# Block 3's first product by seven products too, with seven sums of W_in on GpSimd

## The chip, the cores and the metric

The kernel runs on one core of one Trainium2 chip. The metric is the device time of one execution in microseconds. Before the change it is 192.94 us, the median of three runs (192.56 to 193.59). The engines are named as in the profile: PE is the matmul engine (PEld its weight loads), DVE is VectorE, ACT is ScalarE, POOL is GpSimd, SP is SyncE, which here only issues DMAs.

## The reference

A decayed linear attention (4 batches, 8 heads, 768 positions, head size 64) feeds a two-layer network with the Mish function between its layers:

```
state = gamma * state + k_t (outer) v_t;   y_t = q_t . state / sqrt(64)      # per head
x = y as [3072, 512]
h = x @ w_in        # [512, 2048]
g = h * tanh(softplus(h))
out = g @ w_out     # [2048, 512]
```

The kernel takes and gives float32 and multiplies in float16, with float32 sums in PSUM.

## The kernel before, in words

The 3072 rows are 24 chunks of 128. Block 0 has four chunks (512 rows); blocks 1 to 10 have two each (256 rows). For a block the kernel makes the attention rows, transposed, as the tile `xt`; then the first product `h = x @ w_in` with Mish behind it, which leaves `g`; then the second product `g @ w_out`, whose results go through `osb` to memory. While a block is in its products, PE also makes the scores (`at`), outer products (`u_ps`) and attention outputs (`y_ps`) of the next blocks. All is placed by hand: the order of the calls in the source is the order on every engine's queue, and each queue runs strictly in order.

The second product has two forms. The plain form is one matmul per piece of the inner dimension. The form by seven products (Strassen's scheme in Winograd's variant) cuts each operand into four quarters, makes seven half-size products instead of eight, and needs sums of quarters: of `g` (`gsum`, lines 866 to 879), and of w_out (`tmat`, `weight_sums`, L838). Block 0 uses seven products for half of its inner dimension (`first_out`, L750); its sums of `g` come from `first_sums` (L724) and lie in two of the tiles named `wsum`. Blocks 1 to 3 use `seven` (L985), blocks 4 to 10 `full_out` (L1082).

The first product has two forms too. Blocks 0 to 3 use the plain `g1` (L695): for blocks 1 to 3 eight calls of eight 256-column matmuls, each call followed by one ACT Mish (L714). Blocks 4 to 10 use `full_in` (L905): seven products, in two halves p, each of eight 128-column matmuls, 112 in all (L917). It needs four sums of `xt` (`x_sums`, L899, DVE) and sixteen sums of w_in, four for each of four tiles `wsum` (`in_sums`, L881). In the kernel before DVE makes all sixteen, two in block 1 and seven in each of blocks 2 and 3, one behind each `g1` call named in `SUMS_AT`. `full_in` uses more ACT work than `g1`: copies of partial results out of PSUM (L954, L940) beside the Mish.

The weights come in as float32 and are cast to float16: w_in by `cast_win` (L211; L220 and L226 on DVE, the first piece on POOL and ACT), w_out by `cast_wout` (L239, L241). These casts stand on DVE's queue between the sums of block 0, and PE uses each of them soon after.

POOL's work is the casting and scaling of q, k and v, chunk by chunk (`casts_qk` L437 and L440, `casts_v` L447; for block 1 L317). A one-column copy into `summed` (L1443, L1404) stands ahead of a group of them to hold it back until DVE has made a certain sum. When q and k of a chunk are cast, SP issues a DMA transpose (`turn_by_dma`, L452), whose result `qkt` PE needs for that chunk's scores. SP also issues all loads and nearly all stores, in the order of the calls (`turn_four` L1429 for blocks 2's time, `second_of` L1398 later).

`HALVED` and the variable `wide` in `g1` split some matmuls into two of half the columns, with the weights loaded for each: in block 0 the last seven `g1` calls (28 matmuls of 512 columns become 56 of 256), in block 6 sixteen matmuls of the second product.

Of the kernel before, what the change touches and what calls it, by code (L numbers as in the profile page):

```python
# [9 lines left out]
FP16 = mybir.dt.float16  # L10
# [6 lines left out]
def kernel(  # L17
# [677 lines left out]
    def g1(blk, u):  # L695
        nt = BLOCKS[blk] * C
        per = TB // nt
        h_ps = g1_bank(blk, u)
        for j in range(per):
            s, f = divmod(u * per + j, FPS)  # L700
            for bp in range(NBP):
                wide = 2 * C if u >= NFB - 7 else nt
                for at in range(0, nt, wide):
                    cols = slice(at, at + wide)
                    nc.tensor.matmul(  # L705
                        h_ps[:, j, cols], wins[s][f // 2][:, bp, f % 2 * P:(f % 2 + 1) * P],
                        xts[blk][:, bp, cols], start=(bp == 0 and at == 0), stop=(bp == NBP - 1),
                        skip_group_check=blk == 0)
# [5 lines left out]
        nc.scalar.activation(gt, h_ps, AF.Mish, scale=inv_boost3)  # L714
        for j in range(per):
            gts[blk, u * per + j] = gt[:, j]
# [7 lines left out]
    def first_sums():  # L724
        s = [win_sum_tile(j).rearrange("p a b c -> p (a b) c") for j in range(2)]
        s1, s2, s3, s4 = (s[i // 2][:, i % 2 * FPS:(i % 2 + 1) * FPS] for i in range(4))
        lo, hi = gtiles[0, 0][:, :FPS], gtiles[0, 1][:, :FPS]
        n = TB // 2
        add, sub = ALU.add, ALU.subtract
        return (s1, s2, s3, s4), [  # L730
            lambda: nc.vector.tensor_tensor(s3, lo[:, :, :n], lo[:, :, n:], op=sub),
            lambda: nc.vector.tensor_tensor(s1, lo[:, :, n:], hi[:, :, n:], op=add),
            lambda: nc.vector.tensor_tensor(s2, s1, lo[:, :, :n], op=sub),
            lambda: nc.vector.tensor_tensor(s4, hi[:, :, :n], s2, op=sub),
        ]
# [144 lines left out]

    def in_sums(j):  # L881
        t = win_sum_tile(j)
        (a11, a12), (a21, a22) = [
            (x[:, :2], x[:, 2:]) for x in (wins[j // 2][j % 2], wins[2 + j // 2][j % 2])]
        sub = ALU.subtract
        return [
            lambda: nc.vector.tensor_tensor(t[:, 0], a21, a22, op=ALU.add),
            lambda: nc.vector.tensor_tensor(t[:, 1], t[:, 0], a11, op=sub),
            lambda: nc.vector.tensor_tensor(t[:, 2], a11, a21, op=sub),
            lambda: nc.vector.tensor_tensor(t[:, 3], a12, t[:, 1], op=sub),  # L890
        ]
# [6 lines left out]

    def x_sums(blk, part):  # L899
        ((b11, b12), (b21, b22)), t = x_views(blk)  # L900
        sums = ((t[0], b12, b11), (t[1], b22, t[0]), (t[2], b22, b12), (t[3], b21, t[1]))
        for to, a, b in sums[2 * part:2 * part + 2]:
            nc.vector.tensor_tensor(to, a, b, op=ALU.subtract)

    def full_in(blk, last):  # L905
# [38 lines left out]

        def banks():
            return [single("h_ps", p).rearrange("p (f c) -> p f c", f=n) for p in two]

        pa, pf, m5 = [], [], []
        for p in two:
# [7 lines left out]
            m5.append(kept(pf[p]))  # L957
        if not last:
            u = held[blk + 1][1]
            g = first[blk + 1]  # L960
            for j in range(2):
                us[g + j] = u[:, :, j]
        for p in two:
            mm(pa[p], s(p, 2), t[1])
            nc.vector.tensor_tensor(pf[p], pa[p], m5[p], op=ALU.add)  # L965
            mm(pm[p], a(p, 0, 1), b[1][0])
            mish(p, 0, 0, pm[p])
            if not last:
                (mid_of, state_of)[p](g)
        h22 = []  # L970
        for p in two:
            mm(pa[p], s(p, 3), t[2])
            h22.append(kept(pa[p], m5[p]))
            if not last and p == 1:
# [10 lines left out]
    def seven(blk, masks, hooks):  # L985
# [63 lines left out]
        if blk < ONE:  # L1049
# [10 lines left out]
            call(hooks[2][1:])  # L1060
            mm(pl, a(1, 1), t(4), True)
            done(1, 0, pl, u3)
        else:
            call(hooks[0])
# [7 lines left out]
            mm(pe, s(4), b(1, 1))  # L1072
            x_sums(blk + 1, 0)
# [4 lines left out]
            x_sums(blk + 1, 1)  # L1078
        for i in range(2):
            stores.append((1 + i, out_rows(blk, i), osb[i]))  # L1080

    def full_out(blk, last):  # L1082
# [48 lines left out]
        px = pxps.tile([P, hf], FP32, name="o_ps", tag="px")  # L1131
        halved = HALVED.get(blk, (0, 0))
        mm(px, a(0, 0), b(0, 0), True, halved=halved[0])
# [12 lines left out]
        else:  # L1146
# [5 lines left out]
            pb = bank()  # L1152
            mm(pb, a(0, 1), b(1, 0), True)
            if later is None:
# [16 lines left out]
        done(1, 1, px, m5)  # L1171
        mm(pe, s(4), b(1, 1))
        if not last:
            x_sums(new, 0)
        done(0, 1, pe, u2)
# [4 lines left out]
        cols = slice(0, hf // 2 if last else hf)  # L1180
        mm(px, a(1, 1), t(4), cols=cols)
        if not last:
            x_sums(new, 1)
        done(1, 0, px, cols=cols)
# [28 lines left out]
    def first_block():  # L1213
# [70 lines left out]
        for s in range(1, NSL):  # L1284
            cast_win(s)

        def cast_qk():
# [110 lines left out]
    def second_of(blk):  # L1398
        g = first[blk] + 6
        load, ahead = (load_qk, -1) if blk + 1 == DEFER else (load_to, 0)  # L1400
        if blk != DEFER:
            load(g + 3 + ahead)
        if g < NCK:
            nc.gpsimd.tensor_copy(summed, xts[blk + 1][:, 3, TB - 1:])  # L1404
# [3 lines left out]
            casts_v(g + 1)  # L1408
        if blk == ONE or g >= NCK:
            store_due(NFB)  # L1410
# [65 lines left out]
    for blk in range(1, len(BLOCKS)):  # L1476
# [7 lines left out]
        if blk == 1:  # L1484
            for j in (0, 2, 1, 3):
                input_sums.extend(in_sums(j))
        for u in range(NFB // 2):
            g1(blk, u)
# [6 lines left out]
            elif u in SUMS_AT[blk]:  # L1495
                input_sums.pop(0)()
        later = blk + 2 if blk == ONE else None
        hooks = [([(leave, blk + 1)] if later is not None else []) + [(retain, blk + 1, later)],
# [38 lines left out]
```

## Time and profile before

| | us |
|---|---|
| median of three runs | 192.94 (192.56 to 193.59) |
| the profiled execution, its own time | 192.31 |
| its span, first to last instruction | 190.5 |
| PE busy | 184.8 (97% of the span) |
| DVE busy | 143.1 (75%) |
| ACT busy | 105.8 (56%) |
| POOL busy | 72.2 (38%) |
| mean granted TensorE clock | 0.999 of full speed |

Some 2 us of an execution lie outside the span. Three views are used below. The page gives busy shares and the chain that ended last. The chain in order of time gives the start of each piece, its length and what it was; pieces of one line are merged, and "x48" is the number of instructions. The timeline of an engine gives start, length, line, operation, output and input, the shape and the count; a bracket at the end tells the idle time before the group and what ended it. Matmul starts in the timeline stand some 0.15 us ahead of the chain's, since matmuls overlap.

### The profile page before, as it was taken

What the parts mean: (1) busy time and instruction counts of PE and PEld (TensorE: products, weight loads), DVE (VectorE), ACT (ScalarE), POOL (GpSimd) and SP (SyncE); (2) the same over time, 40 slices, a digit from 0 to 9 for tenths busy, and PEclk for the clock granted to TensorE, in tenths of its full rate; (3) what the DMA queues carried; (4) which work ended last, traced back from release to release, by engine and by line L of the source; (5) the groups of instructions that cost most, each with busy time, mean ns of one, the idle gap of its engine ahead of it and who ended that gap; (6) DMA issues with size and microseconds to landing.
All of it is one profiled execution on the core that took longest, in us unless ns stands there. A gap on an engine that the chain in (4) does not pass through costs nothing.

```text
span 190.5 us, 7643 instructions
## 1 busy us (share of the span) xinstructions
PE 184.8 (97%) x3310; PEld 162.3 (85%) x3310; DVE 143.1 (75%) x294; ACT 105.8 (56%) x201; POOL 72.2 (38%) x100
## 2 busy tenths in 40 slices
PE   7898999999999999999999999999999999999993
PEld 7656478888888888888998998998998998988982
DVE  0778469886977878988798698696697698676862
ACT  3366766264552552553684584584683673873650
POOL 5182000487508745940573634624534710000000
PEclk9999999999999999999999999999999999999999
DMA  4999999999999999899999997891899970301103
GB/s 147 310 303 350 382 387 376 293 330 226 189 237 294 172 235 238 129 266 234 220 186 317 156 202 165 214 200 39 194 174 244 219 172 3 114 3 53 62 3 112
DMA packets 84210, 38.82 MB, mean 204 GB/s; under 512 B 58192, under 2 KB 78288, under 8 KB 84176
## 3 DMA queue, kind: packets, MB, share of 16 engines
q1 hardware_dynamic: 83888, 38.22, 87.1%
q8 instruction: 26, 0.43, 1.0%
q10 hardware_dynamic: 288, 0.11, 0.4%
q14 instruction: 8, 0.07, 0.1%
HBM read 27.31 MB, written 6.29 MB: 176 GB/s over the span
## 4 chain that ended last, share of the span: by engine, by line
PE 93%; DMA 3%; DVE 1%; ACT 1%; issue 0%; SPq 0%; DVEq 0%
PE h_ps L917 23%; PE o_ps L1103 23%; PE h_ps L705 18%; PE o_ps L1007 10%; PE o_ps L762 7%; PE y_ps L609 3%; DMA qfirst<-in_q_dram 3%; PE u_ps L503 1%; PE at L495 1%; PE t_ps L267 1%; PE y_ps L396 1%; PE h_ps L687 1%; PE at L466 1%; PE at L347 1%; DVE qk L279 1%; PE u_ps L368 0%
## 5 line engine op out<-in xcount | busy, mean ns | idle before, releaser
L705 PE MATMUL h_ps<-xt,win 128*128 128x256 f16 (+1 forms) x276 | 34.3, 284 | 0.0
L705 PEld LDWEIGHTS <-win 128*128 128x128 f16 x276 | 26.7, 98 | 6.2 <-DVE win L220 0.3
L714 ACT ACTIVATE g<-h_ps 128x512 f16<-128x512 f32 x38 | 22.7, 597 | 15.2 <-PE h_ps L705 15.2
L917 PE MATMUL h_ps<-xt,wsum 128*128 128x128 f16 x448 | 29.6, 219 | 0.0
L929 ACT ACTIVATE g<-h_ps 128x512 f16<-128x512 f32 x42 | 24.2, 597 | 5.6 <-PE h_ps L917 5.6
L917 PEld LDWEIGHTS <-wsum 128*128 128x128 f16 x448 | 26.2, 98 | 0.0
L917 PE MATMUL h_ps<-xt,win 128*128 128x128 f16 x336 | 24.8, 219 | 0.0
L1103 PEld LDWEIGHTS <-gsum 128*128 128x128 f16 x232 | 21.5, 98 | 2.6
L1103 PE MATMUL o_ps<-tmat,gsum 128*128 128x256 f16 (+1 forms) x176 | 21.5, 268 | 0.0
L917 PEld LDWEIGHTS <-win 128*128 128x128 f16 x336 | 20.8, 98 | 0.2
L440 POOL TENSOR_TENSOR qk<-kf,qvs 128x512 f16<-128x512 f32 x18 | 18.9, 1052 | 2.5 <-DMA kf<-in_k_dram 2.5
L447 POOL TENSOR_TENSOR v<-vf,qvs 128x512 f16<-128x512 f32 x18 | 18.6, 1050 | 2.6 <-DMA vf<-in_v_dram 2.5
L437 POOL TENSOR_TENSOR qk<-qf,qvs 128x512 f16<-128x512 f32 x18 | 19.1, 1062 | 1.3 <-PE u_ps L368 1.3
L1103 PEld LDWEIGHTS <-g 128*128 128x128 f16 x184 | 16.5, 98 | 1.6
L667 ACT CAST xt<-y_ps 128x512 f16<-128x512 f32 x16 | 10.8, 738 | 11.1 <-PE y_ps L609 9.9
L965 DVE TENSOR_TENSOR h_ps<-h_ps,hsum 128x512 f32<-128x512 f32 x14 | 9.7, 695 | 9.2 <-PE h_ps L917 9.1
L1443 POOL COPY summed<-gsum 128x1 f16<-128x1 f16 x7 | 1.6, 233 | 36.8 <-DVE gsum L879 29.4
L954 ACT COPY h_ps<-h_ps 128x512 f32<-128x512 f32 x14 | 8.2, 583 | 12.4 <-issue 8.4
L1103 PE MATMUL o_ps<-wout,g 128*128 128x256 f16 (+1 forms) x120 | 14.5, 265 | 0.0
L1113 ACT COPY snap<-o_ps 128x256 f32<-128x256 f32 (+1 forms) x22 | 8.2, 373 | 11.0 <-PE o_ps L1103 11.0
L1126 DVE TENSOR_TENSOR osb<-o_ps,snap 128x256 f32<-128x256 f32 (+1 forms) x22 | 9.1, 415 | 4.2 <-ACT snap L1113 2.8
L942 DVE TENSOR_TENSOR hsum<-h_ps,hsum 128x512 f32<-128x512 f32 x14 | 9.6, 687 | 0.7 <-PE h_ps L917 0.2
(130 smaller groups left out, 334.0 us busy)
## 6 DMA issues: line engine op xcount, KB each, us to landing
out_dram<-osb SPq DMA_DIRECT2D x22, 256.0 KB, 3.9
qf<-in_q_dram SPq DMA_DIRECT2D x18, 256.0 KB, 4.8
kf<-in_k_dram SPq DMA_DIRECT2D x14, 256.0 KB, 6.0
vf<-in_v_dram SPq DMA_DIRECT2D x14, 256.0 KB, 5.3
wt<-in_moe_w_out_dram SPq DMA_DIRECT2D x6, 512.0 KB, 8.4
vf<-in_v_dram SPq DMA_DIRECT2D x20, 128.0 KB, 3.7
wi<-in_moe_w_in_dram SPq DMA_DIRECT2D x4, 512.0 KB, 8.3
wi<-in_moe_w_in_dram SPq DMA_DIRECT2D x2, 1024.0 KB, 11.1
```

The source lines that it names most:

```text
L437: nc.gpsimd.tensor_tensor(in_place(q16.rearrange("p (w x) d -> p w x d", x=2)), by_head(qf), scale_by_head(qs_two[:, heads]), op=ALU.mult)
L440: nc.gpsimd.tensor_tensor(k16.rearrange("p (y w) d -> p w y d", y=2), kf.rearrange("p (w y) d -> p w y d", y=2), boosts.rearrange("p (w y) ...
L447: nc.gpsimd.tensor_tensor(cast[g][2], loaded.pop(g)[2], vs[g % 2].unsqueeze(2).broadcast_to((P, H, D)), op=ALU.mult)
L667: nc.scalar.copy(dst[:, :, x], src)
L705: nc.tensor.matmul(h_ps[:, j, cols], wins[s][f // 2][:, bp, f % 2 * P:(f % 2 + 1) * P], xts[blk][:, bp, cols], start=(bp == 0 and at == 0) ...
L714: nc.scalar.activation(gt, h_ps, AF.Mish, scale=inv_boost3)
L762: nc.tensor.matmul(banks[ij][:, t], x(f)[:, t * P:(t + 1) * P], w(f), start=ij in open_banks, stop=f == fs[-1], skip_group_check=True)
L917: nc.tensor.matmul(o_ps[:, f], w(f // 2, k)[:, f % 2 * P:(f % 2 + 1) * P], x[:, k], start=begin and f == 0 and k == 0, stop=k == 1, skip_g ...
L929: nc.scalar.activation(gt[:, f:f + n, j * C:(j + 1) * C], src, AF.Mish, scale=inv_boost3)
L965: nc.vector.tensor_tensor(pf[p], pa[p], m5[p], op=ALU.add)
L1007: nc.tensor.matmul(o_ps[:, cols], x(f), w(f)[:, cols], start=first and z == 0, stop=z == n - 1, skip_group_check=True)
L1103: nc.tensor.matmul(o_ps[:, c:c + wide], x(f), w(f)[:, c:c + wide], start=first and f == 0 and c == cols.start, stop=f == n - 1, skip_group ...
```

## The change

- Block 3 is made a block like 4 to 10 in its first product: `full_in` instead of eight `g1` calls (`FULL = (3,)`). In block 3 `full_in` takes its extra PSUM banks from the early pool, carries out the state step of block 3 and the scores of block 4 within it (`both`), and orders its products a little otherwise. Block 2's second product makes block 3's `x_sums` on DVE.
- The sixteen sums of w_in must therefore be made by the end of block 2. DVE makes nine (two in block 1, seven in block 2). POOL makes seven: the four of tile 0 in block 0, right behind its part of the w_in casts and ahead of the casts for block 1, and three in block 1, behind six q, k and v casts.
- The sums of `g` in block 0 move from the `wsum` tiles to a third buffer of `g`, as `wsum` is written earlier.
- The halved matmuls: those of block 0 and block 6 are gone; blocks 4, 5, 7 and 8 get 16, 12, 8 and 24.
- SP's order: in `turn_four` two stores and the five loads of chunk 14 now stand ahead of the transpose of chunk 13; in `second_of` of block 3 two stores stand ahead of the transpose of chunk 15; the deferred loads of v come one block earlier (`DEFER` 5 for 6).

```diff
-    HALVED, DEFER = {6: (8, 8)}, 6
-    SUMS_AT = {1: (4, 5), 2: range(7), 3: range(7)}
+    HALVED = {4: (0, 0, 0, 8, 8), 5: (8, 4, 0, 0, 0), 7: (0, 0, 0, 0, 8), 8: (8, 8, 8, 0, 0)}
+    DEFER = 5
+    FULL, SUMS_AT = (3,), {1: (4, 5), 2: range(7)}
...
-                wide = 2 * C if u >= NFB - 7 else nt
-                for at in range(0, nt, wide):
...
     def first_sums():
-        s = [win_sum_tile(j).rearrange("p a b c -> p (a b) c") for j in range(2)]
-        s1, s2, s3, s4 = (s[i // 2][:, i % 2 * FPS:(i % 2 + 1) * FPS] for i in range(4))
+        s = gp.tile([P, 4, FPS, TB // 2], FP16, name="g", tag="g", bufs=3)
+        s1, s2, s3, s4 = (s[:, i] for i in range(4))
...
-    def in_sums(j):
+    def in_sums(j, on=None):
+        on = on or nc.vector
...
-            lambda: nc.vector.tensor_tensor(t[:, 0], a21, a22, op=ALU.add),
+            lambda: on.tensor_tensor(t[:, 0], a21, a22, op=ALU.add),
...
         def banks():
+            if blk < BACK:
+                t = atps.tile([P, 2, n, C], FP32, name="h_ps", tag="at")
+                return [t[:, p] for p in two]
...
-            mm(pm[p], a(p, 0, 1), b[1][0])
-            mish(p, 0, 0, pm[p])
-            if not last:
+            if not both:
+                mm(pm[p], a(p, 0, 1), b[1][0])
+                mish(p, 0, 0, pm[p])
+            if not settled:
                 (mid_of, state_of)[p](g)
+        if both:
+            leave(blk)
+            for p in two:
+                mm(pm[p], a(p, 0, 1), b[1][0])
+            for p in two:
+                mish(p, 0, 0, pm[p])
...
+        if blk < BACK:
+            get_ready(blk + 1)
         sums_a(blk, 0)
...
@@ in seven()
+            if blk + 1 in FULL:
+                x_sums(blk + 1, slice(0, 1))
...
+            if blk + 1 in FULL:
+                x_sums(blk + 1, slice(1, 4))
...
@@ in first_block()
         for s in range(1, NSL):
             cast_win(s)
+        for make in in_sums(0, nc.gpsimd):
+            make()
...
@@ in second_of()
+        if blk == ONE:
+            store(2)
         if g < NCK:
...
-        if blk == ONE or g >= NCK:
+        else:
             store_due(NFB)
...
@@ in turn_four()
-        for n in (2, 3):
-            casts_v(g + n)
-            turn_by_dma(g + n)
+        casts_v(g + 2)
+        turn_by_dma(g + 2)
         store(2)
+        load_to(g + 5)
+        casts_v(g + 3)
+        turn_by_dma(g + 3)
         load_to(g + 6)
...
@@ the loop over blocks
         if blk == 1:
-            for j in (0, 2, 1, 3):
-                input_sums.extend(in_sums(j))
-        for u in range(NFB // 2):
+            on = [nc.vector] * 2 + [nc.gpsimd] * 3 + [nc.vector] * 7
+            made = {(e, j): in_sums(j, e) for e in on for j in (1, 2, 3)}
+            input_sums.extend(made[e, 1 + m % 3][m // 3] for m, e in enumerate(on))
+        if blk in FULL:
+            full_in(blk, False)
+        for u in range(0 if blk in FULL else NFB // 2):
```

More of the change, by code (lines that the diff above doesn't have):

```diff
@@ L897, in x_views, with x_sums @@
         return b, t
-    def x_sums(blk, part):
+    def x_sums(blk, which):
         ((b11, b12), (b21, b22)), t = x_views(blk)
         sums = ((t[0], b12, b11), (t[1], b22, t[0]), (t[2], b22, b12), (t[3], b21, t[1]))
-        for to, a, b in sums[2 * part:2 * part + 2]:
+        for to, a, b in sums[which]:
             nc.vector.tensor_tensor(to, a, b, op=ALU.subtract)
@@ L973, in full_in @@
             h22.append(kept(pa[p], m5[p]))
-            if not last and p == 1:
+            if not settled and p == 1:
                 mid_of(g + 1)
@@ L1171, in full_out @@
         done(1, 1, px, m5)
-        mm(pe, s(4), b(1, 1))
+        mm(pe, s(4), b(1, 1), halved=halved[3])
         if not last:
-            x_sums(new, 0)
+            x_sums(new, slice(0, 2))
         done(0, 1, pe, u2)
@@ L1496 @@
                 input_sums.pop(0)()
+            if blk == 1 and u == 6:
+                for _ in range(3):
+                    input_sums.pop(0)()
         later = blk + 2 if blk == ONE else None
```

33 lines of the change are left out of this document (17 added, 16 removed).

## The prediction

> **What bounds the kernel now.** I read the shares of the chain that ended last, then that chain in order of time, then the timelines of DVE, PEld and POOL around block 0's weight casts, where the change puts new work, and last SP's around block 3.
>
> ```profile
> PE 93%; DMA 3%; DVE 1%; ACT 1%; issue 0%; SPq 0%; DVEq 0%
> ```
>
> ```profile
> 19.57 12.16 PE h_ps L705 x84
> 31.72 7.15 PE o_ps L762 x64
> 38.88 0.89 PE t_ps L267 x16
> ...
> 77.55 5.24 PE h_ps L705 x48
> ...
> 83.41 1.85 PE h_ps L705 x16
> 85.26 3.50 PE o_ps L1007 x32
> ...
> 89.58 0.32 PE at L495 x32
> ...
> 92.79 6.30 PE h_ps L917 x112
> ...
> 112.86 3.51 PE o_ps L1103 x32
> ...
> 126.63 3.55 PE o_ps L1103 x48
> ```
>
> The chain is PE for 93%, one piece starting where the last ends. So PE work taken out is time gained one for one, and whatever makes PE wait is time lost one for one; nothing later makes it good. How near PE already is to waiting in block 0 is in these rows:
>
> ```profile
> 24.40 0.42 DVE L221 CAST win<-wi 128x512 f16<-128x512 f32 x1
> 24.73 0.69 DVE L226 CAST win<-wi 128x1024 f16<-128x1024 f32 x1
> 26.77 1.29 DVE L226 CAST win<-wi 128x1024 f16<-128x1024 f32 x2 [1.34 <-DMA wi<-in_moe_w_in_dram]
> 27.98 0.68 DVE L731 TENSOR_TENSOR wsum<-g 128x1024 f16<-128x1024 f16 x1
> 28.89 0.69 DVE L732 TENSOR_TENSOR wsum<-g 128x1024 f16<-128x1024 f16 x1 [0.24 <-ACT g L714]
> 29.50 1.22 DVE L241 CAST wout<-wt 128x2048 f16<-128x2048 f32 x1
> ...
> 31.97 1.29 DVE L239 CAST wout<-wt 128x1024 f16<-128x1024 f32 x2
> ...
> 34.90 0.69 DVE L239 CAST wout<-wt 128x1024 f16<-128x1024 f32 x1 [0.44 <-DMA wt<-in_moe_w_out_dram]
> ...
> 36.24 1.53 DVE L856 TENSOR_TENSOR tmat<-wout,wout 128x1024 f16<-128x1024 f16 x1
> ```
>
> ```profile
> 37.82 0.77 PEld L762 LDWEIGHTS <-wsum 128*128 128x128 f16 x8 [0.27 <-DVE tmat L856]
> ```
>
> ```profile
> 16.98 0.61 POOL L220 CAST win<-wi 128x512 f16<-128x512 f32 x1 [3.18 <-DMA wi<-in_moe_w_in_dram]
> 17.53 0.40 POOL L221 CAST win<-wi 128x256 f16<-128x256 f32 x1
> 35.95 2.72 POOL L317 TENSOR_TENSOR qk<-qf,qvs 128x512 f16<-128x512 f32 x2 [18.02 <-DMA qf<-in_q_dram]
> ```
>
> From 26.77 on DVE is all but gapless and feeds PE: the first w_out cast ends at 30.72 and PE takes it at 31.72, 1.0 us later. By 37.82 the slack is gone, PEld waits for the sum of L856. That sum took 1.53 us where L731, of the same shape, took 0.68: it ran beside POOL's pair at 35.95. The same is seen at the end of block 2:
>
> ```profile
> 78.72 1.22 POOL L437 TENSOR_TENSOR qk<-qf,qvs 128x512 f16<-128x512 f32 x1
> ```
>
> ```profile
> 79.30 0.93 DVE L888 TENSOR_TENSOR wsum<-wsum,win 128x512 f16<-128x512 f16 x1
> ```
>
> DVE's sum starts at 79.30, POOL's operation ends at 79.94, and DVE ends 0.29 us after. A DVE sum out of SBUF waits until POOL's running operation is over, then goes ahead of POOL's next. This decides the change.
>
> **The change, part by part.** *First product of block 3.* Removed: 64 matmuls of 256 columns, 5.24 + 1.85 = 7.09 us. Added: 112 of 128 columns, 6.30 us as in block 4. The outer products and scores of block 4 only move. **-0.79 us.**
>
> *Halved matmuls.* 56 halves at 5.24/48 = 0.109 us are 6.11 of block 0's 12.16 us; the other 28 take 6.05, so 0.216 us whole against 0.218 halved: removal gives -0.07 us. In block 6 sixteen halvings cost 3.55 - 3.51 = 0.04, 2.5 ns each; 60 come and 16 go: **+0.11 us.** The bounds are a few hundredths.
>
> *Four sums of w_in on POOL in block 0.* They read the w_in piece that DVE casts until 24.82, so they start then, in what is now POOL's idle 18.02 us. No row has this operation with float16 inputs. The nearest:
>
> ```profile
> L440 POOL TENSOR_TENSOR qk<-kf,qvs 128x512 f16<-128x512 f32 x18 | 18.9, 1052 | 2.5 <-DMA kf<-in_k_dram 2.5
> L814 POOL TENSOR_TENSOR hsum<-hsum 128x512 f32<-128x512 f32 x1 | 1.3, 1277 | 0.0
> ```
>
> I take 1.04 us; the ends are 0.61 (the cast L220, one input) and 1.28 (L814, three wide operands). Whether a DVE cast is held like a sum no row shows either. Ends: not at all, or a whole POOL operation each time. I take the latter, as the casts go from SBUF to SBUF in the sums' time (1.29/2 = 0.65 against 0.68). Then, step by step: POOL waits for DVE's cast at 24.73 to end at 25.42. Its sums one and two run to 27.50; the w_in cast due at 26.77 waits and ends at 28.05 (PE wants it at about 28.2, no loss). Sum three runs to 29.09, the last w_in cast ends at 29.64; sum four to 30.68, DVE's L731 ends at 31.23 and not 28.66. POOL's own next work, the pair of 35.95, waits for its load and is not made later. From 31.23 DVE runs at its present 0.61 us a piece (1.26 for L241): the first w_out cast ends at 33.10, not 30.72. PE, ready at 31.65, waits 1.5 us. The casts of row 31.97 now end at 34.9 and 35.5 and cost PE 0.25. Then POOL's pair of 35.95 no longer meets L856 alone but the two last w_out casts, which end at 37.7 and 39.3; PE, which got there at 36.9, waits 0.9 and 0.7 for the halves. L856 now follows at 40.5 without a wait. PE reaches the transposes at 42.2 and not at 38.88: **+3.4 us** against the present schedule, the -0.07 included. With POOL at 0.61 us the same steps leave 0.4, at 1.28 about 4.6.
>
> The Trainium skill (SBUF — State Buffer, Who interferes with whom) states that GpSimd and VectorE share one port pair held for a whole instruction, and that copies and casts in a two-port mode contend as two-input sums do. By it the sum is as I have it; if only the sums were held, as far as the trace shows, the block-0 loss would be the 0.3 us of the second rival. L856's 1.53 us agrees; no run here shows it for a cast.
>
> *Three sums on POOL in block 1.*
>
> ```profile
> 49.35 1.19 POOL L447 TENSOR_TENSOR v<-vf,qvs 128x512 f16<-128x512 f32 x1 [0.26 <-DMA vf<-in_v_dram]
> 57.98 0.52 POOL L1443 COPY summed<-gsum 128x1 f16<-128x1 f16 x1 [7.44 <-DVE gsum L875]
> ```
>
> They fit the 7.44 us idle, 3.1 us of it; nothing queued behind them comes later. Cost 0; without that cover the casts behind, and the transposes, would be up to 3.1 us late.
>
> *DVE and ACT in blocks 2 and 3.* DVE loses seven sums in block 3 and gets four `x_sums` at the end of block 2:
>
> ```profile
> L903 DVE TENSOR_TENSOR xt<-xt 128x256 f16<-128x256 f16 x28 | 7.7, 296 | 0.9 <-ACT xt L667 0.3
> ```
>
> `full_in` is 14 groups of eight matmuls, 0.45 us each. The first `x_sums` is wanted by its second group, the second by its fifth, 1.8 us in; at 0.3 us each they come in time, and the DVE work queued behind them (results into `osb`) has no PE waiting. ACT's chain in block 4 ends here:
>
> ```profile
> 99.30 1.08 ACT L929 ACTIVATE g<-h_ps 128x512 f16<-128x512 f32 x2
> ```
>
> that is 1.3 us behind PE's end at 99.09. In block 3 PE wants its last half 1.3 us after, but block 4's scores, 0.6 us, now stand inside `full_in` and give ACT that room. Cost 0, at most 0.6. Moving block 0's sums of `g` to a third buffer of `g` costs nothing: block 1's `g` then reuses the buffer that block 0's last products do not read.
>
> *SP's order.* Chunk 13's transpose, last of these two, falls behind two stores and five loads:
>
> ```profile
> 79.95 3.43 SPq L452 DMA_TRANSPOSE qkt<-qk  x2
> 83.48 1.05 SPq L1372 DMA_DIRECT2D out_dram<-osb  x2
> 84.58 0.51 SPq L169 DMA_DIRECT2D qf<-in_q_dram  x1
> 85.15 1.86 SPq L169 DMA_DIRECT2D kf<-in_k_dram  x2
> 87.05 1.05 SPq L169 DMA_DIRECT2D vf<-in_v_dram  x2
> ```
>
> ```profile
> DMA to landing us min/median/max: 3.1/4.3/6.3
> ```
>
> It is issued 88.10 - 83.48 = 4.6 us later, at about 86.7, and lands at 91.0. PE wants it for the scores at 89.58, in the second half of that piece, and 0.8 us earlier with the shorter block 3. On an undisturbed PE that is a wait of about 2 us, 0 to 3.5. With PE 3.4 us late already, POOL's casts and SP wait for the same DVE sums as PE while the loads ahead have had 3.4 us more to drain, so the 2 us are covered: 0 taken, up to 2. The other moved stores (1.05 us per pair) and the earlier `DEFER` stand before transposes that land by the same gates; 0, up to 0.5.
>
> **Sum.** 3.4 - 0.79 + 0.11 = **+2.7 us**. The profiled execution took 192.31, so 195.0; it was 0.63 below the median of the runs shown, 192.94, against which the time is **195.6 us** (+1.4%). This case's own range, from POOL's 0.61 and 1.28: 192.6 to 196.9.
>
> **Rivals.** *The sums hide and the transpose lands in time* (the other side). Place: POOL between 24.8 and DVE's gapless stretch. If POOL takes under about 0.6 us a sum, or DVE's casts pass it, PE waits for nothing: -0.79 - 0.07 + 0.11 = -0.75, 192.2. For it: DVE idles 1.34 us at 25.42. Against: even POOL's one-input cast took 0.61. It decides when four sums end before DVE's L731 at 27.98.
>
> *Only two-input sums are held.* Casts keep their times; L731, L732 and L856 each wait part of a POOL operation, and PE loses about 0.3 us in block 0. PE is then nearly on time at the scores of block 5 and meets the late transpose: 0.3 + 1.6 - 0.75 = +1.1, 194.1. For it: only sums are seen stretched. Against: no cast of the trace runs beside POOL, so that is no evidence.
>
> *Block 3 gains nothing,* because its thinner covers (ACT's Mish, `x_sums`) hold PE for the 0.8 us saved, on top of the first case: 196.4. Against: seven blocks run the same 6.30 us.
>
> **Chances.** Forecast 0.50, hidden 0.27, sums only 0.16, no gain 0.07. 0.5% is 0.96 us, about what a measurement can tell from no change. Hidden is -0.4%: mostly "same", with 0.08 of it over the line. The forecast's low end and part of the second rival are "same" too, 0.10. So faster 0.08, same 0.29, slower 0.63. The range 192.1 to 197.0 holds all but the outer ends.
>
> **What would show it.** Right: in the new profile DVE's w_in casts at 27 to 30 us last over 1 us, PE or PEld waits for `wout` near 32 and again near 37, and `h_ps` of block 3 takes about 6.9 us with block 4's scores. Wrong: these casts at 0.65 us beside POOL's sums, POOL's float16 sums well under 1 us, or a wait at `qkt` before block 5's scores.

## The result, and the profile after

The changed kernel takes 201.94 us (median of six runs, 200.01 to 203.15) against 192.90 for the kernel before: a ratio of 1.042, 95% interval 1.036 to 1.048. It is slower, as forecast, but by 9 us where 2.7 were forecast, and outside the range. Run again later, it took 203.36 and 204.40. The ratios leave out the two longest runs both of the changed kernel (203.10 and 203.15) and of e5_turn_alone below (196.66 and 197.48, of which the last has the profile).

The profiled execution took 200.01 us, its span is 198.2 (before: 192.31 and 190.5). The shares of its chain by engine:

```profile
PE 71%; DVE 12%; DMA 11%; issue 2%; SPq 2%; ACT 0%; DVEq 0%
```

PE no longer carries the chain alone (it had 93%). Where others take over is in the chain in order of time (start, length, what):

```profile
26.30 3.00 DVE win L227 x2
29.31 1.56 DVE g L728
...
35.74 2.91 DVE wout L240 x2
38.70 2.78 PE o_ps L759 x24
41.48 0.89 PE t_ps L268 x16
...
80.71 0.46 PE h_ps L915 x8
81.19 0.62 PE h_ps L915 x8
81.85 1.96 PE h_ps L915 x32
83.86 0.35 issue
84.20 1.28 DVE h_ps L968 x2
...
89.84 4.88 DMA qkt<-qk
94.76 0.38 PE at L496 x24
...
97.99 6.30 PE h_ps L915 x112
...
111.58 0.27 issue
...
153.90 0.64 issue
```

There are four kinds of loss in it: block 0 (the transposes start at 41.48, were at 38.88); block 3, whose first product (80.71) now meets DVE's work and then the landing of chunk 13's transpose; short stops named "issue", in which PE waits for no semaphore; and, behind the chain, the end of the program. The table gives, for all kernels of this document, the time in us from the first matmul of a block's first product to that of the next block, from PE's timeline; "end" is from the last matmul's end to the end of the span.

| kernel | 0 | 1 | 2 | 3 | 4 | 5 | 6 | 7 | end |
|---|---|---|---|---|---|---|---|---|---|
| before | 30.13 | 14.78 | 14.84 | 15.23 | 13.77 | 13.77 | 13.88 | 13.67 | 3.1 |
| changed | 33.28 | 15.09 | 15.09 | 17.28 | 14.25 | 14.12 | 13.84 | 14.49 | 3.9 |
| e11, changed again | 33.20 | 15.09 | 15.08 | 21.19 | 13.81 | 13.80 | 13.84 | 14.65 | 4.0 |
| e1_pool4 | 33.19 | 14.77 | 14.84 | 15.24 | 13.77 | 13.98 | 14.24 | 13.67 | 3.1 |
| e5_turn_alone | 30.21 | 14.78 | 14.96 | 20.40 | 13.77 | 13.78 | 14.21 | 13.67 | 3.1 |
| e6_halved_alone | 30.11 | 14.77 | 15.46 | 15.23 | 13.78 | 13.80 | 14.47 | 13.67 | 4.1 |
| e2_sums0_dve | 30.57 | 16.28 | 15.40 | 16.82 | 15.16 | 13.80 | 13.84 | 14.39 | 4.0 |
| e3_turn_order | 33.16 | 15.08 | 15.40 | 15.91 | 14.37 | 13.80 | 13.84 | 14.33 | 4.0 |
| e4_both | 31.49 | 15.28 | 15.09 | 15.32 | 14.56 | 13.89 | 13.83 | 15.31 | 4.1 |
| e7_casts_behind | 31.44 | 15.52 | 15.09 | 14.91 | 15.57 | 13.80 | 13.84 | 14.21 | 4.0 |
| e8_no_halves | 31.43 | 15.55 | 15.32 | 14.90 | 14.02 | 14.30 | 13.84 | 13.67 | 4.0 |
| e9_sums_placed | 30.27 | 14.77 | 15.87 | 14.90 | 13.93 | 14.46 | 13.84 | 14.38 | 3.4 |
| e10_defer | 30.10 | 14.78 | 15.59 | 14.91 | 13.83 | 14.73 | 13.84 | 13.67 | 4.0 |

For the first profile of the changed kernel the differences are +3.15 in block 0, +0.56 in blocks 1 and 2, +2.05 in block 3, +1.61 in blocks 4 to 7, +0.08 behind them, +0.8 at the end, and -0.55 before block 0's first product, which the trace of before reached that much later; together 7.7, the difference of the spans.

Block 0, in the timelines of POOL and DVE:

```profile
24.45 1.52 POOL L885 TENSOR_TENSOR wsum<-win 128x512 f16<-128x512 f16 x1 [7.07 <-DVE win L222]
26.05 1.15 POOL L886 TENSOR_TENSOR wsum<-wsum,win 128x512 f16<-128x512 f16 x1
27.16 1.60 POOL L887 TENSOR_TENSOR wsum<-win,win 128x512 f16<-128x512 f16 x1
28.72 1.60 POOL L888 TENSOR_TENSOR wsum<-win,wsum 128x512 f16<-128x512 f16 x1
```

```profile
26.30 3.00 DVE L227 CAST win<-wi 128x1024 f16<-128x1024 f32 x2 [1.34 <-DMA wi<-in_moe_w_in_dram]
29.23 1.64 DVE L728 TENSOR_TENSOR g<-g 128x1024 f16<-128x1024 f16 x1
```

The two casts take 3.00 us and took 1.29; each ends some 0.55 us after one of POOL's sums (the second at 29.31, POOL's third sum at 28.76). So casts are held like sums, and POOL's own sums are stretched too, to 1.15 to 1.60 us. The rule that the prediction drew from the Trainium skill (SBUF — State Buffer, Who interferes with whom), that casts contend too, holds here.

### The profile page after: what moved, and what is told of

It is laid out like the page before. It is cut to its first block, busy times and chain, and to the rows that moved or that the text cites. A ratio compares the mean times of both kernels' runs of the same rounds, so it can differ in the third digit from the quotient of the medians.

```text
span 198.2 us, 7794 instructions
## 1 busy us (share of the span) xinstructions
PE 186.5 (94%) x3374; PEld 160.2 (81%) x3374; DVE 148.6 (75%) x295; ACT 107.3 (54%) x205; POOL 81.1 (41%) x107
## 4 chain that ended last, share of the span: by engine, by line
PE 71%; DVE 12%; DMA 11%; issue 2%; SPq 2%; ACT 0%; DVEq 0%
PE h_ps L915 24%; PE o_ps L1120 22%; PE h_ps L703 6%; DMA wi<-in_moe_w_in_dram 6%; PE o_ps L1019 6%; PE o_ps L759 5%; PE y_ps L610 3%; DMA qfirst<-in_q_dram 3%; DMA qkt<-qk 2%; DVE wout L240 2%; DVE win L227 2%; SPq L170 1%; PE t_ps L268 1%; PE at L496 1%; PE at L467 1%
## 5 line engine op out<-in xcount | busy, mean ns | idle before, releaser
L915 PE MATMUL h_ps<-xt,wsum 128*128 128x128 f16 x512 | 33.6, 219 | 0.3 <-DVE h_ps L968 0.3
L927 ACT ACTIVATE g<-h_ps 128x512 f16<-128x512 f32 x48 | 27.6, 596 | 6.9 <-PE h_ps L915 6.9
L915 PEld LDWEIGHTS <-wsum 128*128 128x128 f16 x512 | 29.9, 98 | 0.6 <-issue 0.4
L915 PE MATMUL h_ps<-xt,win 128*128 128x128 f16 x384 | 28.2, 219 | 0.7 <-issue 0.6
L703 PE MATMUL h_ps<-xt,win 128*128 128x256 f16 (+1 forms) x184 | 27.1, 305 | 0.1
L915 PEld LDWEIGHTS <-win 128*128 128x128 f16 x384 | 23.6, 98 | 1.2 <-issue 1.0
L703 PEld LDWEIGHTS <-win 128*128 128x128 f16 x184 | 17.7, 98 | 8.4 <-DVE win L227 0.7
L711 ACT ACTIVATE g<-h_ps 128x512 f16<-128x512 f32 x30 | 17.9, 597 | 11.5 <-PE h_ps L703 11.5
L968 DVE TENSOR_TENSOR h_ps<-h_ps,hsum 128x512 f32<-128x512 f32 x16 | 11.0, 694 | 10.6 <-PE h_ps L915 10.5
L1120 PEld LDWEIGHTS <-g 128*128 128x128 f16 x216 | 17.2, 98 | 1.8 <-issue 0.4
L955 ACT COPY h_ps<-h_ps 128x512 f32<-128x512 f32 x16 | 9.3, 584 | 15.0 <-issue 10.0
L759 PEld LDWEIGHTS <-g 128*128 128x128 f16 x120 | 11.3, 98 | 5.0 <-DVE wout L242 1.7
L759 PE MATMUL o_ps<-wout,g 128*128 128x256 f16 x88 | 10.9, 273 | 2.2 <-DVE wout L242 1.2
```

The source lines that it names most:

```text
L703: nc.tensor.matmul(h_ps[:, j], wins[s][f // 2][:, bp, f % 2 * P:(f % 2 + 1) * P], xts[blk][:, bp, :nt], start=(bp == 0), stop=(bp == NBP - 1))
L759: nc.tensor.matmul(banks[ij][:, t], x(f)[:, t * P:(t + 1) * P], w(f), start=ij in open_banks, stop=f == fs[-1], skip_group_check=True)
L915: nc.tensor.matmul(o_ps[:, f], w(f // 2, k)[:, f % 2 * P:(f % 2 + 1) * P], x[:, k], start=begin and f == 0 and k == 0, stop=k == 1, skip_g ...
L927: nc.scalar.activation(gt[:, f:f + n, j * C:(j + 1) * C], src, AF.Mish, scale=inv_boost3)
L1120: nc.tensor.matmul(o_ps[:, c:c + wide], x(f), w(f)[:, c:c + wide], start=first and f == 0 and c == cols.start, stop=f == n - 1, skip_group ...
```

## The experiments

Each time is given against that of the kernel before, run beside it, with their ratio and its 95% interval. The code cuts show the main lines of each edit.

**One part of the change alone: e1_pool4, e5_turn_alone, e6_halved_alone**

```diff
+        for make in in_sums(0, nc.gpsimd):      # e1: before, tile 0's sums on POOL
+            make()
...
+        casts_v(g + 2)                          # e5: before, turn_four as changed
+        turn_by_dma(g + 2)
+        store(2)
+        load_to(g + 5)
+        casts_v(g + 3)
+        turn_by_dma(g + 3)
...
-    HALVED, DEFER = {6: (8, 8)}, 6              # e6: before, halved matmuls as changed
+    HALVED = {4: (0, 0, 0, 8, 8), 5: (8, 4, 0, 0, 0), 7: (0, 0, 0, 0, 8), 8: (8, 8, 8, 0, 0)}
-                wide = 2 * C if u >= NFB - 7 else nt
+                wide = nt
```

> The kernel before with one part of the change: the four sums of tile 0 of W_in are made on GpSimd in block 0, where the change puts them, and DVE makes the other twelve in blocks 1 to 3. If the sums on POOL hold DVE's casts and sums of block 0, as the trace of the changed kernel has it, this kernel is 2.5 to 3.2 us longer than before, the transposes of L267 start about 41.5 instead of 38.88, and DVE's w_in and w_out casts beside POOL last about 1.5 us instead of 0.65. Rival: the stretch of block 0 comes from something else that the change does there (its whole 512-column matmuls, the new places of the sums of g): then this kernel is within 0.5 us of before.

Measured: 195.52 against 192.82 us, 1.014 (1.010 to 1.018), +2.7. This kernel also has the third buffer of `g`, which the early sums need. Block 0 is 3.06 longer, blocks 1 to 4 are as before. PE waits where forecast:

```profile
PE o_ps L762 <- DVE wout L241: 1.2, 1, 1.2
PE o_ps L762 <- DVE wout L239: 1.0, 2, 0.6
```

The rows are PE's waits (total, times, longest). The sums on POOL make block 0's loss; the buffer does not, since e9 below has it too and its block 0 is as before.

> The kernel before with one part of the change: in the turn of chunks 12 to 15, two stores and the five loads of chunk 14 stand ahead of chunk 13's transpose. The prediction took 0 for this, as covered by a late PE, and 2 us (0 to 3.5) on an undisturbed PE; here PE is undisturbed. If the late transpose is a cost of its own, PE waits at qkt ahead of the scores that stood at 89.58, 1.8 to 3 us, and the kernel is as much longer than before. Rival: the wait of the changed kernel came from the delays ahead of it; then this kernel is within 0.4 us of before.

Measured: ten runs from 192.75 to 197.48, median 194.37 against 192.50; 1.008 (1.004 to 1.011). The order costs on an undisturbed PE, in the median, what the prediction had put there (1.9 us, forecast about 2), and it varies from run to run by almost 5 us. The profile is of the longest run; its chain, then its stretches (width, busy time with counts of PE, PEld, DVE, ACT, POOL, and then the granted clock):

```profile
87.77 5.12 DMA qkt<-qk
```

```profile
89.00:93.00 4.00, 0.44 (x41) 0.34 (x35) 0.76 (x2) 0.00 (x0) 2.18 (x3) 0.97 1.03 198
93.00:95.00 2.00, 2.00 (x47) 1.57 (x47) 0.00 (x0) 1.27 (x2) 0.00 (x0) 0.50 0.92 206
95.00:98.00 3.00, 3.00 (x29) 2.50 (x28) 2.16 (x6) 0.04 (x1) 0.00 (x0) 0.80 1.11 247
```

PE stands from 89.18 to 92.93 (3.75 us between two matmul starts), and behind that runs at half its clock, then recovers: 2 x (4 x 0.03 + 2 x 0.50 + 3 x 0.20) = 3.4 us at half clock. So this wait is paid for a second time: block 3 is 5.2 us longer, 1.4 more than the wait.

> The kernel before with one part of the change: block 0's and block 6's halved matmuls whole again, and 60 matmuls of blocks 4, 5, 7 and 8 halved. The computation and everything on the other engines are as before. By the matmuls' own times this is +0.04 us. The theory of the instruction lines: PE's instructions arrive in packets of 256, one is asked for when PE enters the line ahead of it, so a line that PE uses up in less than some 4.2 us holds it. Counting the instructions, in this kernel the lines that cover the attention matmuls of block 3's and block 6's second products are used up in about 2.7 and 2.0 us (the shortest of before takes 3.6). So PE stands still twice: about 1 to 2 us behind block 3's scores (line's end at instruction 2753, within the outputs y_ps), and 2 to 3 us in block 6's second product (instruction 4545), 3 to 5 us in all, with no semaphore waited for. Rival, and the prediction's step: within 0.3 us of before.

Measured: 194.21 against 192.50, 1.009 (1.006 to 1.013), +1.7. The prediction's step, +0.04, is wrong. So is the size that the theory gave: there is one stop, not two, of 0.5 and not 2 to 3 us. But it is at the predicted instruction, in the middle of block 6's second product:

```profile
131.63 0.21 PE o_ps L1104
131.85 0.46 issue
132.31 2.68 PE o_ps L1104 x23
```

In its profile the stop makes block 6 0.6 longer; 0.6 more lie in block 2, where a DVE sum of `g` takes 1.26 us beside a POOL cast and took 0.41 before (a small shift decides whether the two meet), and 1.0 at the end, of which more below. Against that its block 0 begins 0.4 sooner, as in every trace but that of before.

**Parts of the change undone: e2_sums0_dve, e3_turn_order, e4_both**

```diff
-        for make in in_sums(0, nc.gpsimd):      # e2, e4: four sums on DVE, one behind
-            make()                              # weight(0, 1), three ahead of y_two()
...
-        casts_v(g + 2)                          # e3, e4: turn_four as before
-        turn_by_dma(g + 2)
+        for n in (2, 3):
+            casts_v(g + n)
+            turn_by_dma(g + n)
         store(2)
-        load_to(g + 5)
-        casts_v(g + 3)
-        turn_by_dma(g + 3)
         load_to(g + 6)
```

> The changed kernel with tile 0's four sums made on DVE in block 0, one between two w_in casts and three behind the last w_out sum, and none on POOL there. If the sums on POOL are worth 3 us in block 0, this kernel gains 2.5 to 3.3 us on the changed one and PE reaches the transposes at 38.5 to 39.2. Since PE is then early at block 3 again, a second theory (what was taken as cover in block 0 hides part of chunk 13's late transpose) has the wait at qkt grow from 1.8 us to over 3, and the gain falls to about 1.5; the theory that the wait moves with PE keeps it at 1.5 to 2.2 us.

Measured: 200.55 (198.93 to 203.62), 1.039 (1.029 to 1.050). PE reaches the transposes at 38.44, yet by the medians only 1.4 us are gained, where 2.5 to 3.3 were expected: the sums that I put on DVE beside POOL's casts are held themselves, DVE falls behind, and block 1 becomes 1.2 us longer (16.28 against 15.09). The wait for the transpose stays, with 0.9 us in the profile of the shortest run; that fits neither theory (1.5 to 2.2, or over 3). The two longer runs (202.03 and 203.62) have the lower mean clock again, 0.991 and 0.979. This experiment replaced one collision by another; e9 does it properly.

> The changed kernel with SP's order of before in the turn of chunks 12 to 15: chunk 13's transpose ahead of the two stores and chunk 14's loads. If the late transpose is what costs block 3 its gain, the wait at qkt of 1.8 us is gone, block 3 to block 4 becomes 2.0 to 2.8 us shorter, and the time is 1.8 to 2.8 us below the changed kernel's. Rival: block 3's seven products are themselves longer (ACT's copies and x_sums hold PE), and the wait at qkt only stands in for that: then at most 0.5 us is gained and the wait turns up at h_ps.

Measured: 198.72 against 192.82, 1.030 (1.024 to 1.035), by the two ratios 2.4 us less than the changed kernel, as expected, and the spread of 3 us is down to 2. The wait at qkt is gone, block 3 is 17.28 - 15.91 = 1.4 us shorter than in the changed kernel's first profile. It is still 0.7 longer than before: the rival has a share in it.

> The changed kernel with both: tile 0's sums on DVE and SP's old order. If the two causes add, it gains 4.5 to 6 us on the changed kernel, some 194 to 196. What is then left against the kernel before, less the 0.8 us that block 3 should save, is due to something else: the theory is that PE now waits for its own instructions in three or four places in blocks 4 to 8, 0.3 to 0.6 us each, as in the changed kernel at 111.6, 123.1 and 153.9 us; in blocks 4 to 8 this kernel then is still 1 to 1.7 us longer than before. Rival: those losses come from the late schedule (loads and stores that collide because PE is 5 us late), and go with it: then this kernel ends at 192.2, 0.7 us below before.

Measured: 197.22 against 192.82, 1.021 (1.017 to 1.026). By the ratios it gains 4.0 us on the changed kernel, a little less than expected: the wait for chunk 13's transpose goes, but of block 0's 3.15 us 1.36 are left, since the sums on DVE are held there as in e2. Against the kernel before 4.4 us remain. Blocks 4 to 7 are together 2.5 us longer than before, where 1 to 1.7 were expected, so those losses do not go with the late schedule. Block 3 takes 15.32, so its seven products save nothing. Why is in DVE's timeline there, beside POOL's:

```profile
78.65 0.92 DVE L905 TENSOR_TENSOR xt<-xt 128x256 f16<-128x256 f16 x1
...
80.15 2.56 DVE L905 TENSOR_TENSOR xt<-xt 128x256 f16<-128x256 f16 x3
82.64 1.28 DVE L972 TENSOR_TENSOR h_ps<-h_ps,hsum 128x512 f32<-128x512 f32 x2
```

```profile
79.38 1.09 POOL L448 TENSOR_TENSOR v<-vf,qvs 128x512 f16<-128x512 f32 x1
80.43 1.09 POOL L438 TENSOR_TENSOR qk<-qf,qvs 128x512 f16<-128x512 f32 x1
81.48 1.09 POOL L441 TENSOR_TENSOR qk<-kf,qvs 128x512 f16<-128x512 f32 x1
```

Three sums of `xt` at 0.3 us take 2.56: one per POOL cast. The add behind them (L972) starts at 82.64, and PE waits for it.

**That hold taken away: e7_casts_behind**

```diff
+                nc.gpsimd.tensor_copy(summed, xts[blk + 1][:, 3, TB - 1:])  # behind x_sums
+                behind.pop()()      # casts of q, k and transpose of chunk 13, then as before
...
-        if blk == ONE:              # second_of as before
-            store(2)
```

> The changed kernel with tile 0's sums on DVE in block 0, all of SP's order of before around block 3, and one thing more: POOL's casts of q and k of chunk 13 wait until DVE has made block 3's four sums of xt. In the run with both undone, those sums took 0.92 and 2.56 us (three) beside POOL's casts, where 0.3 each is usual, the add of L972 started 0.6 us late, and block 3 gained nothing. If DVE's sums held by POOL are what eats block 3's gain, they now end 1 to 1.5 us earlier, PE's first product of block 3 with the state step takes about 7.1 us and not 7.8, the wait at qkt in block 4 (0.4 us) is gone with SP's old order, and the time is 0.7 to 1.2 us below that run's. Rival: ACT's copies out of PSUM hold PE in block 3; then block 3 stays at 7.6 to 7.8 us. The stalls without a wait in blocks 4 and 7 stay in both cases, 1 to 2 us.

Measured: 197.30 against 192.50, 1.024 (1.020 to 1.028). The mechanism is as expected for three of the four sums, which run free. The first does not; it stands beside a POOL cast as before:

```profile
78.77 0.92 DVE L905 TENSOR_TENSOR xt<-xt 128x256 f16<-128x256 f16 x1
79.61 0.74 DVE L1038 TENSOR_TENSOR osb<-o_ps,snap 128x256 f32<-128x256 f32 x2
80.27 0.86 DVE L905 TENSOR_TENSOR xt<-xt 128x256 f16<-128x256 f16 x3
```

Block 3 is 14.91, 0.4 shorter than in e4 and 0.3 shorter than before. Of the 0.79 us forecast 0.5 are still missing, and 0.4 of that shows here: PE's second group of eight matmuls, at 79.74, waits for the first sum, and the third, at 80.40, for the results into `osb`, which DVE makes late and which free its PSUM bank. Each starts 0.2 us late. The total is not better, since block 4 took the gain and more. There PE stopped for 1.6 us with no semaphore to wait for:

```profile
107.76 1.58 issue
```

**The stops without a wait: e8_no_halves**

```diff
-    HALVED = {4: (0, 0, 0, 8, 8), 5: (8, 4, 0, 0, 0), 7: (0, 0, 0, 0, 8), 8: (8, 8, 8, 0, 0)}
+    HALVED = {}
```

> The kernel of e7_casts_behind with one thing changed: no matmul of blocks 4 to 8 is halved (60 were). By the matmuls' own times -0.15 us. The run e6_halved_alone had its stall exactly at the predicted instruction (4545), but 0.5 us long and not 2 to 3, and none at 2753. The traces so far give a better rule for the instruction lines: the packet for a line starts 0.4 to 2.9 us (median 1.75) after PE reaches a place some 30 instructions ahead of the line before it, takes 1.2, and its first instruction runs 1.45 us after its end; so 286 instructions must last some 3.1 to 5.5 us. By it the stalls of block 4's second product (1.6 us in e7_casts_behind) and ahead of block 8 (0.4) go, and new ones of 0 to 0.7 us may come in block 5's second product (instruction 4033) and at the start of block 9 (5825): 1 to 1.8 us faster than e7_casts_behind. Rival: the stalls belong to those stretches of time (transfers that delay the packets) and not to the count: they stay in block 4 and ahead of block 8, and no more than 0.3 us is gained.

Measured: 195.50 against 192.49, 1.016 (1.013 to 1.019), 1.8 us below e7. Blocks 4 and 7 lose their stops (15.57 to 14.02, 14.21 to 13.67), and a new one of 0.6 comes in block 5's second product, at instruction 4033 as said; none comes at 5825. How the counting goes: PE's instructions are numbered in the order of its queue, a weight load and a matmul being two, and the few that wait for a semaphore or drain the engine one each. The page counts 26 packets on the queue for its instructions:

```profile
q8 instruction: 26, 0.43, 0.9%
```

That is 16 KB each, and one for every 256 of PE's 6600 to 6760 instructions; an instruction line is such a group of 256. In eleven of the thirteen profiles (of twelve kernels) PE stops in blocks 4 to 8, 19 times in all, for 0.34 to 1.80 us with no semaphore and always at an instruction numbered 193 plus a multiple of 256 (193 is read off the stops themselves):

```
kernel            stops: instruction (us between matmul starts, us from the packet's end to the restart)
before            none; least time from a packet's end to its line's first instruction 1.62
changed           3521 (0.49, 1.50)  4033 (0.38, 1.45)  5313 (0.86, 1.47)
e1_pool4          4033 (0.41, 1.49)
e2_sums0_dve      3521 (1.40, 1.60)  5313 (0.39, 1.46)
e3_turn_order     3521 (0.61, 1.32)  5313 (0.70, 1.64)
e4_both           3521 (0.44, 1.56)  5313 (1.68, 1.56)
e5_turn_alone     4545 (0.39, 1.38)
e6_halved_alone   4545 (0.74, 1.33)
e7_casts_behind   3521 (1.80, 1.55)  5313 (0.57, 1.50)
e8_no_halves      4033 (0.63, 1.39)
e9_sums_placed    3521 (0.49, 1.41)  4033 (0.34, 1.34)
e10_defer         3521 (0.49, 1.52)  4033 (0.61, 1.53)
changed again     none; least time 1.61
```

Each stop ends 1.3 to 1.65 us after the end of a packet on that queue; where the time was longer, there was none. All thirteen traces, that of before too, have one more such stop in block 0's start, at instruction 449 = 193 + 256, of 0.1 to 0.7 us; in the trace of before it is the wait "PE y_ps L396 <- issue: 0.5". It is common to all of them and makes no difference between kernels. The lines concerned are those that hold the small attention matmuls: PE takes 3.0 to 4.7 us for such a line and the 30 instructions ahead of it. e1 has PE's instructions of the kernel before, in the same order, and stops where that did not, and the changed kernel stops three times in one profile and not at all in the other: the packets' delays differ from run to run, and a halving moves the line ends onto other work. What delays a packet was not settled.

**The sums of W_in placed anew: e9_sums_placed, e10_defer**

```diff
         for s in range(1, NSL):
             cast_win(s)
+            if s == 2:
+                for make in in_sums(0):      # on DVE, ahead of the last casts
+                    make()
...
-    DEFER = 5                                # e10 only
+    DEFER = 6
```

> The kernel of e8_no_halves with the sums of W_in placed anew: tile 0's four on DVE ahead of the last w_in casts, where DVE waits 1.34 us for the transfer; two of tile 1 in DVE's idle places at 39.2 and 44.3 us; in block 1 two on DVE and one on POOL that needs no other sum (before: three, two of which started at 54.0 and held gsum); seven in block 2. If sums on POOL, or on DVE beside POOL, are what makes blocks 0 and 1 longer (1.15 and 0.74 us in e7_casts_behind), these two come within 0.4 us of before, and the time is 1.2 to 1.7 us below e8_no_halves. Rival: full products of 512 columns or the earlier loads make them longer: then it stays within 0.4 us of e8_no_halves.

Measured: 194.54, 1.011 (1.007 to 1.016), 1.0 us below e8, a little less than expected. Blocks 0 and 1 are at 30.27 and 14.77, as before the change. DVE makes the four sums in the gap of 1.34 us, and the casts have their old length:

```profile
25.96 0.42 DVE L891 TENSOR_TENSOR wsum<-win,wsum 128x512 f16<-128x512 f16 x1
26.30 1.29 DVE L227 CAST win<-wi 128x1024 f16<-128x1024 f32 x2
```

Block 2 took half a microsecond more than in e8, with the hold of a `g` sum that e6 has too. The 14.38 of block 7 hold a wait of 0.7 us at `qkt`.

> The kernel of e9_sums_placed with the deferred loads of v where they were before the change (block 6, not 5). The prediction took 0, up to 0.5 us, for the earlier loads. If these loads delay the instruction packets or the transposes in block 4 and 5, this kernel is 0.3 to 1 us faster than e9_sums_placed and its stalls in blocks 4 and 5 are gone; if they are hidden, the two agree within 0.3 us.

Measured: 194.25, 1.008 (1.006 to 1.010). Within 0.3 us of e9: the earlier loads of v cost nothing that shows in the medians, and the stops in block 5 stay. The wait at `qkt` in e9's block 7 is gone; such waits of 0.4 to 1.0 us, in block 4 or 7, stand in four of the eight profiles with `DEFER` at 5 and in none of the five with 6. Whether the loads make them was not settled. This is the best kernel with block 3 by seven products, and it is slower than the kernel before: block 3 gives back 0.3, while stops for instructions cost about 1 in block 5, block 2 0.75 and the end 0.9. No version here beats the kernel before.

**The spread: e11_changed_again**

This is the changed kernel once more, with nothing altered.

> The changed kernel once more, unchanged, for another profile. Four of its six runs had a mean granted clock of 0.987 to 0.989 and took 200.8 to 203.2 us, where the profiled one had 0.996 and 200.01. In e5_turn_alone's profile a wait of 3.75 us at qkt was followed by 2 us at a granted clock of 0.50 and 3 us at 0.80. Theory: the wait of the changed kernel at qkt (1.8 us in its profile) differs from run to run with the transpose's landing, and where it gets longer than some limit between 1.8 and 3.7 us PE's clock is halved for the next few us, which costs 1 to 1.5 us more. If this profile has a mean clock of 0.99 or less, the lower clock stands right behind the wait at qkt in block 3 and that wait is over 2.5 us. Rival: the lower clock stands behind block 0's waits (1.6 us at 31 us) or is spread over the run, and is no matter of the transposes.

Measured: 203.36 for the profiled run, mean clock 0.987, and the lower clock stands right behind the wait, as the theory had it. PE's wait, SP's queue ahead of the transpose, and the stretches behind it:

```profile
PE at L496 <- DMA qkt<-qk: 4.9, 2, 4.1
```

```profile
89.12 2.59 SPq L170 DMA_DIRECT2D vf<-in_v_dram  x2
91.82 1.49 SPq L453 DMA_TRANSPOSE qkt<-qk  x1
```

```profile
92.00:94.00 2.00, 0.84 (x88) 0.73 (x81) 1.18 (x3) 0.33 (x1) 0.57 (x2) 1.00 0.93 143
94.00:96.00 2.00, 0.00 (x0) 0.00 (x0) 0.00 (x0) 0.00 (x0) 1.61 (x2) 1.00 1.09 108
96.00:98.00 2.00, 1.04 (x43) 0.82 (x43) 0.00 (x0) 0.45 (x1) 0.00 (x0) 0.84 1.03 207
98.00:100.00 2.00, 2.00 (x12) 1.43 (x10) 0.62 (x2) 0.87 (x2) 0.00 (x0) 0.50 1.31 223
100.00:104.00 4.00, 4.00 (x55) 3.66 (x54) 2.73 (x8) 1.65 (x4) 0.58 (x2) 0.90 1.32 253
```

The loads that now stand ahead of the transpose took 1.5 us longer to issue, the transpose left at 91.82 instead of 89.84, PE waited 4.1 us, and then ran 2 x (2 x 0.16 + 2 x 0.50 + 4 x 0.10) = 3.4 us at half clock, as in e5. Block 3 takes 21.19 us, 6 more than before; no stop for instructions occurs in blocks 4 to 8 of this run (the 14.65 of block 7 hold a wait of 1.0 us at `qkt`). Why the loads took longer to issue was not settled. Four of the first six runs have the same low mean clock; that they waited likewise is inferred, since they have no trace.

## Why the prediction was wrong, step by step

- **Four sums on POOL in block 0, +3.4:** right in mechanism and size. +3.15 and +3.07 in the two profiles, +2.7 for the whole kernel in e1. PE's waits for `wout`, forecast at 1.5 and 1.6 us, are 1.2 and 1.0. POOL's sum takes 1.15 to 1.6 us; 1.04 was taken.
- **SP's order, "0 taken, up to 2":** the step that failed. The side reckoning, about 2 us on an undisturbed PE, was borne out by e5's median; its range, 0 to 3.5, was not (block 3 is 5.2 longer in e5's longest run). The argument that PE's lateness covers the wait was wrong. The prediction knew that POOL's casts and SP's queue hang on the same DVE sums as PE, and counted on the loads ahead to drain while PE is late. But a transpose that hangs on the same sums moves with PE, and the time to drain bought nothing. PE starts block 3 at 80.71 (3.16 later), and the transpose is issued at 89.84, 3.1 later than the 86.7 worked out for an undisturbed PE. It took 4.9 us to land, just as in the kernel before, where it was issued at 82.14:

```profile
82.14 1.24 SPq L452 DMA_TRANSPOSE qkt<-qk  x1
```

  The wait is 1.8 us in one profile and 4.1 in the other, and behind the longer one comes a second term that the prediction lacked, the halved clock (e5 and e11). Together block 3 loses 1.4 (17.28 - 15.91) to 5.3 us (21.19 - 15.91) by it. In the longer profile this is the largest miss; in the first one the missing gain of block 3 and the stops are each as large.
- **First product of block 3, -0.79, with DVE and ACT at 0:** PE's own work was reckoned rightly, but not the cover. The prediction put the sums of `xt` at 0.3 us each from blocks 4 to 10; at the end of block 2 POOL is casting, and they take 0.9 each. It had shown this very hold at 79.30, at the end of block 2, and applied it to block 0 alone. It also said that PE waits for none of the results into `osb`, and in e7 PE does, 0.2 us. With the hold on all four sums nothing is gained (e4), with three of them free 0.3 us (e7), and beside the rest of the change block 3 is 0.7 longer (e3).
- **Three sums on POOL in block 1, 0:** +0.3. Two of them come late, behind a DVE sum, and hold the sums of `g`:

```profile
55.49 2.56 POOL L886 TENSOR_TENSOR wsum<-wsum,win 128x512 f16<-128x512 f16 x2 [2.90 <-DVE wsum L885]
```

  With one sum on POOL that waits for nothing, block 1 is as before (e9).
- **Halved matmuls, +0.04 in all (-0.07 and +0.11):** failed. The matmuls' own time is right (block 0 is 0.02 shorter in e6), but the number of instructions moves the ends of PE's instruction lines. In e6 the kernel lost 1.7; 0.6 of it is the stop, the rest lies in block 2 and at the end, and only the stop was foreseen by the counting. 60 halved matmuls less are worth 1.8 us in e8 against e7. In the changed kernel's first profile the three stops account for the 1.61 in blocks 4 to 7 (0.43, 0.37 and 0.80 beyond the usual time between starts, 0.06 us or, among the small matmuls, 0.01).
- **The end, no term:** 0.8 us. The last store, from ACT's queue, landed 1.7 us after its issue before and 2.5 in the changed kernel (the two rows, in this order):

```profile
out_dram<-osb ACTq DMA_DIRECT2D x1, 64.0 KB, 1.7
out_dram<-osb ACTq DMA_DIRECT2D x1, 64.0 KB, 2.5
```

- **`DEFER` and the third buffer of `g`, 0:** right as far as the medians show (e10 against e9; block 0 in e9).

The forecast's sign and its largest term stood. Of the 9 us, some 2.4 had no term at all (stops 1.6 and end 0.8 in the first profile), and 1.4 to 5.3 were a term that was reckoned rightly and then argued away. The second rival had the transpose's wait, but only with block 0's loss nearly gone. The third, that block 3 gains nothing, came true beside the forecast's block 0; it was given a chance of 0.07. None named the stops or the end.

## What to carry to other kernels

A wait is covered by a late engine only if what it waits for does not hang on the same gate; look for the gate of each before setting the cost at nothing. Where one shared hold (here POOL over DVE) is found, look for it in every stage where the moved work lands. And where PE runs many small matmuls, count its instructions: a change that costs nothing in matmul time can move the end of a group of 256 into the densest stretch.

## What the runs showed of the hardware

- **PE waits for its instructions.** In blocks 4 to 8 of these traces a line of 256 is usable 1.3 to 1.65 us after its packet ends, and a line that with the 30 instructions ahead of it lasts 3.0 to 4.7 us can be too short for the next packet; the stops are 0.3 to 1.8 us long and different from run to run. The Trainium skill (Runtime: NRT & Kernel Launch, Instruction fetch mechanics) has the blocks of 256 and calls the cost of crossing one mostly hidden. In blocks 4 to 8 that holds for two of the thirteen profiles, that of before and the second of the changed kernel, and not for the other eleven.
- **After a long wait PE ran at half its clock.** After waits of 3.75 and 4.1 us PE had 3.4 us at half clock; after 1.8 us it stayed at 1.00. The Trainium skill (TensorE: Matmul & The Clock Gate, Part 1: The HAM clock gate) gives about 3.4 us for the window after which an idle PE is halved, and for the busy one that frees it; the runs agree with both, and by themselves put the limit between 1.8 and 3.75.
- **The last store can be late.** Where it landed after some 2.5 us, its last packets of 512 B came behind one 8 KB instruction packet of queue 14 (in the changed kernel at 195.96 to 196.53 us); where it landed after 1.7 that packet came last. By the table's last column it was late in all kernels with another number of PE instructions than before, least in e9 (2.0 us to landing). Why was not found.
